# Unit 8's x by the DMA crossbar and the sinks' rows of v by four GpSimd transfers, with a rewritten order of work

## The chip, the cores and the metric

The kernel runs on one core of one Trainium2 chip. Five engines work side by side: TensorE (PE) multiplies matrices, VectorE (DVE) and ScalarE (ACT) work element by element, GpSimd (POOL) does the same more slowly and can issue transfers, and SyncE (SP) issues most transfers. The metric is the device time of one execution in microseconds. The profile is of one execution, taken by the hardware profiler.

## The reference

Two parts follow each other. The first is attention with a window and sinks, for 4 batches (called images below), 8 heads, 768 positions and 64 channels per head. A query sees the keys of its own and the 127 positions before it, and the first 4 positions of the sequence, the sinks:

```python
scores = scale * np.matmul(q, k.transpose(0, 1, 3, 2))
keep = is_sink | in_window          # is_sink: pos < 4; in_window: 0 <= q - k < 128
a = softmax(np.where(keep, scores, -1e9))
attn_out = np.matmul(a, v)          # heads side by side: x, [4, 768, 512]
```

The second is a channel mix with a hidden width of 1024:

```python
xk = mu_k * x + (1 - mu_k) * x_prev      # x_prev: x one position earlier
xr = mu_r * x + (1 - mu_r) * x_prev
k = np.maximum(xk @ w_k, 0)
out = sigmoid(xr @ w_r) * ((k * k) @ w_v)
```

## The kernel before

The work is cut into 12 units of 256 positions, three for each image: unit u is third `T = u % 3` of image `b = u // 3`. A unit passes through four functions.

- `prepare` (line 528) casts q, k and v from f32 to bf16 and turns q and k so that channels lie on partitions. For units in the lists `KD` and `QD` the turn is a crossbar transpose that SP issues (line 562); for the others it is four PE transposes into a PSUM bank (line 576) and an evacuation by ACT or DVE (line 589). For the first unit of an image it also makes the sinks' keys and values.
- `attend` (line 686) makes scores (line 721), exponentials (ACT, line 775), the mask (DVE, line 789), the product with v (PE, line 808), the reciprocal and the scaled x (DVE, lines 822 and 825). In units 0 and 1, which are in `BIAS`, the mask is added by products with `ident` (line 728). In the second and third unit of an image the sinks come in by scores with `ksink` (line 696), an exponential (line 703) and a product with `vsink` (line 763).
- `mix` (line 834) turns x. For units in `XD` SP issues two crossbar transposes (line 869); for the others it is two halves of four PE transposes each (line 849) and two evacuations (line 858). Then DVE makes the difference `td` of x and x one position earlier (line 877) and the mixes xk and xr, eight instructions (line 888).
- `ffn` (line 928) makes the key products with w_k (line 939), relu (lines 949 or 953), the square (lines 963 or 967), the gate with w_r (line 979) and tanh (line 985), the product with w_v (line 997), the output (line 1006) and the store (line 1013). The last 128 positions go in two column halves (`last_product`, lines 909 to 924).

**The sinks' values before.** `vsink` is a [128, 8 heads, 65] tile that is zero except in the rows where a head finds its four sink positions. A PE product of v's first 128 rows with the constant `spread` (line 676) brings the four sink rows of v to those partitions in a PSUM bank, and DVE multiplies the bank by the mask `hmask` into `vsink` (line 680). Both happen once for each image. `spread` is made by POOL from `ident` (line 451). The keys' counterpart `ksink` is filled by POOL copies (line 670).

**The order.** Each engine works through its own queue in order. The program first records every operation with a number (`Plan.op`), and then emits them in the order of the table `ORDER`. A negative number there is a fill: a product of zeros (line 1018) into a bank that is free at that place. `CHOICE` names the engine where an operation could go to more than one, and `SLOTS` the buffer for each tile. Nothing is decided while the kernel runs; a queue stands still until its next instruction's inputs and buffers are there. SP's queue holds the loads, the crossbar transposes and the stores in one order, so that a transpose that waits for its input keeps what stands behind it waiting.

Of the kernel before, what the change touches and what calls it, by code (L numbers as in the profile page):

```python
# [18 lines left out]
    92: "ACT", 93: "ACT", 94: "ACT", 95: "ACT", 97: "ACT", 100: "ACT", 102: "DVE", 105: "DVE",  # L19
    110: "DVE", 111: "DVE", 114: "ACT", 115: "DVE", 139: "POOL", 142: "POOL", 145: "POOL", 148:  # L20
    "DVE", 150: "DVE", 151: "ACT", 152: "ACT", 154: "DVE", 161: "DVE", 191: "DVE", 193: "DVE",
    194: "DVE", 197: "DVE", 199: "DVE", 200: "DVE", 203: "DVE", 204: "DVE", 213: "DVE", 230:
    "ACT", 234: "ACT", 273: "DVE", 276: "DVE", 279: "DVE", 282: "DVE", 285: "ACT", 286: "ACT",
    298: "DVE", 306: "DVE", 315: "ACT", 354: "DVE", 364: "ACT", 365: "DVE", 367: "DVE", 383:
    "ACT", 387: "ACT", 436: "DVE", 439: "DVE", 444: "DVE", 445: "DVE", 467: "ACT", 475: "ACT",
    514: "DVE", 516: "DVE", 521: "DVE", 524: "ACT", 525: "ACT", 546: "ACT", 550: "ACT", 554:
    "ACT", 558: "ACT", 595: "DVE", 598: "DVE", 603: "ACT", 604: "ACT", 606: "DVE", 634: "ACT",
    681: "DVE", 682: "DVE", 691: "DVE", 700: "ACT", 704: "ACT", 708: "ACT", 755: "DVE", 759:
    "DVE", 760: "ACT", 772: "DVE", 781: "ACT", 785: "ACT", 789: "ACT", 834: "DVE", 836: "DVE",
    837: "DVE", 853: "ACT", 856: "DVE", 857: "ACT", 860: "DVE", 861: "ACT", 904: "DVE", 906:  # L30
    "DVE", 910: "DVE", 912: "DVE", 913: "DVE", 929: "ACT", 933: "ACT", 940: "DVE", 941: "ACT",
    994: "DVE", 995: "ACT", 999: "ACT", 1003: "ACT", 1007: "ACT", 1022: "DVE", 1026: "DVE",
    1034: "DVE", 1035: "ACT",
# [5 lines left out]
XD = (9,10,11)  # L39
# [146 lines left out]
def kernel(  # L186
# [209 lines left out]

    xts = [tile1([128, NC, S + 16], BF16, f"xt{i}") for i in range(2)]
    ones = tile1([128, 128], BF16, "ones")

    def fill():  # L400
        for t, value in ((ones, 1.0), (spread, 0.0), (hmask, 1.0)):
            nc.vector.memset(t, value)
# [672 lines left out]
```

## Time and profile before

| | |
|---|---|
| median of 3 runs | 166.04 us (165.84 to 166.12) |
| span of the profiled execution | 164.3 us; no other time of this execution is given |
| PE busy | 158.4 us, 96% |
| DVE busy | 145.4 us, 89% |
| ACT busy | 131.2 us, 80% |
| POOL busy | 13.5 us, 8% |
| mean granted TensorE clock | 0.999 |

The span runs from the first to the last instruction. In a group of instructions, the line, the engine and the operation come first, then the tiles written and read, the count, the busy time in us, the mean ns of one, and the idle time of the engine ahead of them with what ended it. In a timeline, the first two numbers are the start and the length in us. Busy times of PE are modelled to each matmul's end, and matmuls overlap, so the distance from one start to the next tells what a matmul holds PE for.

### The profile page before, as it was taken

To read this page: it belongs to the slowest core of one execution; us is meant where nothing else is said; L and a number is where in the kernel's file an instruction comes from. 1 tells how busy PE (TensorE), PEld (TensorE's weight loads), DVE (VectorE), ACT (ScalarE), POOL (GpSimd) and SP (SyncE) were. 2 spreads that over 40 slices of the span, in tenths; PEclk is the share of its full clock that TensorE was granted. 3 is DMA by queue.
4 is the path that set the end of the run, shared out by engine and by line. 5 is a ranking of instruction groups with operands and counts; after the bars stand their busy time and mean duration, and the time that the engine had idled before them with its cause. 6 is when DMAs were issued, how large, how long until landed. Compare 5 with 4: busy or idle time off the path is not lost.

```text
span 164.3 us, 4195 instructions
## 1 busy us (share of the span) xinstructions
PE 158.4 (96%) x1603; PEld 102.6 (62%) x1603; DVE 145.4 (89%) x381; ACT 131.2 (80%) x218; POOL 13.5 (8%) x38
## 2 busy tenths in 40 slices
PE   6999889999999999999999999999999999999992
PEld 2455568866467587577566775856575765664851
DVE  5259999999999999989999999999999999789752
ACT  3277999999999999999999999997668759163240
POOL 6409300010000000060000000000000000000000
PEclk9999999999999999999999999999999999999999
DMA  4999999999969896999999887986996955077743
GB/s 120 247 305 311 348 335 355 301 354 210 228 154 270 135 240 148 234 198 167 224 216 157 188 156 163 235 146 150 199 123 136 362 149 200 0 90 297 262 185 128
DMA packets 79042, 34.60 MB, mean 211 GB/s; under 512 B 67112, under 2 KB 73520, under 8 KB 79024
## 3 DMA queue, kind: packets, MB, share of 16 engines
q1 hardware_dynamic: 79008, 34.35, 86.3%
q8 instruction: 12, 0.20, 0.6%
q14 instruction: 6, 0.05, 0.1%
q10 hardware_dynamic: 16, 0.00, 0.0%
HBM read 24.12 MB, written 6.29 MB: 185 GB/s over the span
## 4 chain that ended last, share of the span: by engine, by line
PE 79%; ACT 8%; SPq 4%; DMA 3%; issue 2%; DVE 1%; POOL 1%; DVEq 0%; ACTq 0%; POOLq 0%
PE bank L997 23%; PE bank L939 23%; PE bank L979 12%; PE bank L808 6%; PE sc L721 6%; SPq L337 3%; DMA qs<-in_q_dram 3%; PE bank L576 2%; ACT e L775 2%; PE bank L849 2%; ACT rl L949 1%; PE bank L763 1%; ACT qt L589 1%; PE bank L909 1%; PE bank L1018 1%
## 5 line engine op out<-in xcount | busy, mean ns | idle before, releaser
L775 ACT ACTIVATE e<-sc 128x1024 bf16<-128x1024 f32 (+1 forms) x48 | 46.1, 994 | 1.8 <-PE sc L721 1.7
L939 PE MATMUL bank<-xk,wk_sb 128*128 128x256 bf16 x384 | 47.1, 273 | 0.0
L997 PE MATMUL bank<-wv_h,kk 128*128 128x512 bf16 x184 | 43.1, 379 | 0.1
L939 PEld LDWEIGHTS <-wk_sb 128*128 128x128 bf16 x384 | 36.4, 98 | 7.4 <-issue 0.4
L949 ACT ACTIVATE rl<-bank 128x512 bf16<-128x512 f32 x40 | 24.2, 625 | 8.6 <-PE bank L939 7.1
L997 PEld LDWEIGHTS <-kk 128*128 128x128 bf16 x184 | 17.1, 98 | 17.8 <-issue 0.4
L789 DVE TENSOR_TENSOR e<-e,mask 128x1024 bf16<-128x1024 bf16 (+1 forms) x40 | 25.4, 642 | 0.7 <-ACT e L775 0.5
L979 PE MATMUL bank<-wr_sb,xr 128*128 128x512 bf16 x96 | 23.7, 379 | 0.0
L888 DVE SCALAR_TENSOR_TENSOR xk<-td,mu_all,xt 128x256 bf16<-128x256 bf16 x48 | 22.4, 483 | 0.3
L888 DVE SCALAR_TENSOR_TENSOR xr<-td,mu_all,xt 128x256 bf16<-128x256 bf16 x48 | 22.1, 475 | 0.2
L967 ACT ACTIVATE kk<-rl 128x512 bf16<-128x512 bf16 x29 | 18.3, 664 | 4.2 <-DVE rl L953 4.0
L985 ACT ACTIVATE th<-bank 128x512 f32<-128x512 f32 x24 | 15.1, 646 | 5.7 <-PE bank L979 5.7
L825 DVE TENSOR_TENSOR x<-bank,rec 128x256 bf16<-128x256 f32 x48 | 19.2, 416 | 0.4
L808 PE MATMUL bank<-vb,e 128*128 128x65 bf16 x352 | 16.6, 194 | 0.0
L1006 DVE SCALAR_TENSOR_TENSOR w<-th,bank 128x512 f32<-128x512 f32 x19 | 13.0, 682 | 3.6 <-issue 1.8
L808 PEld LDWEIGHTS <-e 128*128 128x128 bf16 x352 | 13.6, 97 | 3.5
L979 PEld LDWEIGHTS <-xr 128*128 128x128 bf16 x96 | 8.8, 98 | 8.6 <-issue 0.2
L721 PE MATMUL sc<-qt,kt 64*128 64x128 bf16 (+1 forms) x256 | 13.9, 238 | 0.0
L721 PEld LDWEIGHTS <-kt 64*128 64x128 bf16 x256 | 8.9, 94 | 5.7 <-issue 3.1
L1018 PE MATMUL bank<-warm 128*128 128x512 bf16 x30 | 10.6, 484 | 1.1 <-DVE warm L1038 1.1
L877 DVE TENSOR_TENSOR td<-xt 128x512 bf16<-128x512 bf16 x24 | 10.3, 428 | 0.7 <-ACT xt L858 0.5
L589 ACT COPY qt<-bank 128x512 bf16<-128x512 bf16 x15 | 9.4, 643 | 1.0 <-PE bank L576 1.0
(74 smaller groups left out, 161.7 us busy)
## 6 DMA issues: line engine op xcount, KB each, us to landing
ks<-in_k_dram SPq DMA_DIRECT2D x24, 256.0 KB, 4.7
qs<-in_q_dram SPq DMA_DIRECT2D x24, 256.0 KB, 4.4
vs<-in_v_dram SPq DMA_DIRECT2D x24, 256.0 KB, 4.4
out_dram<-w SPq DMA_DIRECT2D x19, 256.0 KB, 2.7
w<-in_moe_w_k_dram SPq DMA_DIRECT2D x2, 1024.0 KB, 10.4
w<-in_moe_w_v_dram SPq DMA_DIRECT2D x2, 1024.0 KB, 9.3
w<-in_moe_w_r_dram SPq DMA_DIRECT2D x1, 1024.0 KB, 9.7
out_dram<-ob SPq DMA_DIRECT2D x4, 256.0 KB, 2.6
```

Source lines behind the costliest of these rows:

```text
L721: nc.tensor.matmul(out=sc[:, a, o0:o1], lhsT=lhs[rows], rhs=rhs[rows], start=u not in BIAS, stop=True, skip_group_check=u in BIAS)
L775: nc.scalar.activation(out=buf[ek][:, :, lo:], in_=buf[sck][:, :, lo:], func=AF.Exp, scale=scale)
L789: nc.vector.tensor_tensor(out=at, in0=at, in1=m, op=ALU.mult)
L808: nc.tensor.matmul(out=o[:, g, a, :], lhsT=e[:, a, e0:e0 + 128], rhs=rhs, start=(T == 0 and i == 0), stop=(i == len(blocks) - 1), skip_gro ...
L825: P.op("DVE", dve(256), lambda ok=ok, rk=rk, c=c: nc.vector.tensor_tensor(out=buf["x", u][:, :, 128 * c:128 * c + 128].rearrange("p g (a d ...
L888: nc.vector.scalar_tensor_tensor(out=buf[key][:, c, :], in0=buf[tk][:, i, :], scalar=mu[w][:, c:c + 1], in1=xt[:, c, t0 - 1:t0 + 255], op0 ...
L939: nc.tensor.matmul(out=ps[:, i, :], lhsT=wk_sb[:, c, 128 * f:128 * f + 128], rhs=xk[:, c, :], start=(c == 0), stop=(c == NC - 1), skip_gro ...
L949: nc.scalar.activation(out=buf[rk], in_=buf[psk].rearrange("p (i t) -> p i t", i=2), func=AF.Relu)
L967: nc.scalar.activation(out=buf["kk", u][:, 2 * f2:2 * f2 + 2, :], in_=buf[rk], func=AF.Square)
L979: nc.tensor.matmul(out=buf[psk], lhsT=buf["xr", u][:, c, 128 * g:128 * g + 128], rhs=wr_sb[:, c, :], start=(c == 0), stop=(c == NC - 1))
L985: P.op("ACT", act(512), lambda psk=psk, tk=tk: nc.scalar.activation(out=buf[tk], in_=buf[psk], func=AF.Tanh, scale=0.5), rank + 4 + g, tak ...
L997: nc.tensor.matmul(out=buf[psk], rhs=wv_h[:, f, :], lhsT=buf["kk", u][:, f, 128 * g:128 * g + 128], start=(f == 0), stop=(f == NF - 1))
```

## The change

- `XD` takes in unit 8. Its x is turned by two crossbar transposes that SP issues, and its eight PE transposes and two evacuations are gone.
- `spread` and the four products with it are gone. A new tile `vstage` (f32, [128, 4, 64]) is set to zero by DVE, and then four transfers issued by POOL write the sinks' rows of v for all four images at once: transfer i brings position i of every head and image to partitions i, i + 16, and so on, 8 partitions and 32 rows of 256 bytes. `vsink` is the product of `vstage` (spread over the heads) and `hmask`, read from SBUF; it can go to POOL or DVE, and `CHOICE` gives all four to DVE. `hmask` and `ksink` follow the new places of the rows (16 apart for the two heads of a pair, not 4).
- The sinks' keys of image 1 are followed by 18 POOL writes of zero, of one element per partition, to an unused tile `spare`.
- `ORDER`, `CHOICE` and `SLOTS` are rewritten. SP loads q ahead of k for units 0 and 1. Fills go from 30 to 24. On POOL, units 0 and 1 get three more casts (half of v of unit 0, both of unit 1). Of the relus 2 are on DVE, where 8 were; of the squares 26, where 19 were; of v's casts 7, where 13 were; of q's casts 8, where 14 were. The first and the last quarter of w_k are cast by DVE, where all four were ACT's.

The core of the diff (the three tables are left out; their effect stands above):

```diff
-XD = (9,10,11)
+XD = (8, 9, 10, 11)
...
-    spread = tile1([128, 128], BF16, "spread")
...
+    vstage = tile1([128, B, D], FP32, "vstage")
...
+    spare = tile1([128, 18], FP32, "spare")
...
-        for t in ksink + vsink:
+        for t in ksink + vsink + [vstage]:
             nc.vector.memset(t, 0.0)
...
-            keep(m, -4 * a, [[-32, NP], [0, D + 1]], 1, m)
-            keep(m, 3 + 4 * a, [[32, NP], [0, D + 1]], -1, m)
+            keep(m, -16 * a, [[-32, NP], [0, D + 1]], 1, m)
+            keep(m, 3 + 16 * a, [[32, NP], [0, D + 1]], -1, m)
...
+    for i in range(NS):
+        P.op("POOL", 1000.0, lambda i=i: nc.gpsimd.dma_start(
+            out=vstage[i::16], in_=v[:, :, i, :].rearrange("b h d -> h b d")), -50,
+            service=60.0, descs=32, reads=["stage0"], writes=[("vstage", i)])
...
-                nc.gpsimd.tensor_copy(out=kz[rows, :, 4 * a:4 * a + NS],
+                nc.gpsimd.tensor_copy(out=kz[rows, :, 16 * a:16 * a + NS],
                                       in_=first(rows))
+            if b == 1:
+                for i in range(18):
+                    nc.gpsimd.memset(spare[:, i:i + 1], 0.0)
...
-        psk = ("vsp", b)
-        P.op("PE", 220.0, lambda: nc.tensor.matmul(
-            out=buf[psk].rearrange("p (h d) -> p h d", h=H), lhsT=spread,
-            rhs=buf["vb", u][:, 0, :, 0:D], start=True, stop=True), rank + 4, lag=PE_LAG,
...
-        P.op("DVE", dve(512), lambda: nc.vector.tensor_tensor(
...
+        def sink_values(engine):
+            return lambda: engine.tensor_tensor(
+                out=vsink[b % 2][:, :, 0:D], op=ALU.mult, in1=hmask[:, :, 0:D],
+                in0=vstage[:, b, :].unsqueeze(1).to_broadcast([128, H, D]))
+
+        P.op("POOL", 1250.0, sink_values(nc.gpsimd), rank + 4, port=True,
+             alts={"POOL": (1250.0, sink_values(nc.gpsimd), True),
+                   "DVE": (dve(512), sink_values(nc.vector), True)},
+             reads=[("vstage", i) for i in range(NS)] + ["hmask", "sinks"],
+             writes=[("vsink", b % 2)])
```

More of the change, by code (lines that the diff above doesn't have):

```diff
@@ L18 @@
 CHOICE = {
[L19 to L30, printed above, removed]
@@ L31 @@
-    "DVE", 910: "DVE", 912: "DVE", 913: "DVE", 929: "ACT", 933: "ACT", 940: "DVE", 941: "ACT",
-    994: "DVE", 995: "ACT", 999: "ACT", 1003: "ACT", 1007: "ACT", 1022: "DVE", 1026: "DVE",
-    1034: "DVE", 1035: "ACT",
+    95: "DVE", 96: "ACT", 97: "ACT", 98: "DVE", 99: "DVE", 100: "ACT", 101: "DVE", 102: "DVE",
+    103: "ACT", 104: "DVE", 105: "DVE", 107: "ACT", 108: "ACT", 110: "DVE", 111: "DVE", 113:
+    "DVE", 114: "ACT", 116: "ACT", 117: "DVE", 118: "POOL", 120: "DVE", 141: "POOL", 143: "ACT",
@@ new lines @@
+    144: "DVE", 146: "ACT", 147: "POOL", 149: "ACT", 150: "POOL", 152: "ACT", 153: "POOL", 154:
+    "POOL", 156: "DVE", 163: "DVE", 193: "DVE", 195: "ACT", 196: "DVE", 198: "ACT", 199: "DVE",
+    201: "DVE", 202: "ACT", 204: "ACT", 205: "DVE", 206: "ACT", 208: "ACT", 215: "ACT", 223:
+    "ACT", 224: "ACT", 227: "ACT", 228: "DVE", 231: "DVE", 232: "ACT", 235: "ACT", 236: "ACT",
+    275: "DVE", 277: "ACT", 278: "DVE", 280: "ACT", 281: "DVE", 283: "ACT", 284: "DVE", 286:
+    "ACT", 287: "ACT", 288: "ACT", 290: "DVE", 292: "DVE", 299: "DVE", 307: "ACT", 308: "DVE",
@@ new lines @@
+    311: "ACT", 312: "DVE", 315: "ACT", 316: "ACT", 319: "ACT", 320: "DVE", 355: "DVE", 357:
+    "ACT", 359: "ACT", 360: "ACT", 362: "ACT", 364: "ACT", 365: "ACT", 366: "DVE", 368: "DVE",
+    375: "ACT", 383: "ACT", 384: "ACT", 387: "ACT", 388: "ACT", 391: "ACT", 392: "DVE", 395:
+    "ACT", 396: "DVE", 435: "ACT", 437: "DVE", 439: "ACT", 440: "DVE", 442: "ACT", 444: "ACT",
+    445: "DVE", 446: "DVE", 448: "ACT", 455: "DVE", 463: "ACT", 464: "DVE", 467: "ACT", 468:
+    "DVE", 471: "ACT", 472: "DVE", 475: "ACT", 476: "ACT", 515: "ACT", 517: "ACT", 519: "ACT",
@@ L34 @@
+    934: "ACT", 937: "ACT", 938: "DVE", 991: "ACT", 992: "ACT", 995: "DVE", 996: "DVE", 999:
+    "ACT", 1000: "DVE", 1003: "ACT", 1004: "DVE", 1019: "ACT", 1020: "DVE", 1023: "ACT", 1024:
+    "DVE", 1027: "ACT", 1028: "ACT", 1031: "ACT", 1032: "DVE",
 }
@@ L395 @@
     vsink = [tile1([128, H, D + 1], BF16, f"vsink{i}") for i in range(2)]
+    vstage = tile1([128, B, D], FP32, "vstage")
     xts = [tile1([128, NC, S + 16], BF16, f"xt{i}") for i in range(2)]
     ones = tile1([128, 128], BF16, "ones")
+    spare = tile1([128, 18], FP32, "spare")
     def fill():
-        for t, value in ((ones, 1.0), (spread, 0.0), (hmask, 1.0)):
+        for t, value in ((ones, 1.0), (hmask, 1.0)):
             nc.vector.memset(t, value)
@@ L414 @@
     const_op("DVE", 500.0, fill, ["ones0"], rank=-80)
-    const_op("DVE", 1800.0, fill_later, ["sinks0", "ones", "edges"], rank=-79)
+    const_op("DVE", 1800.0, fill_later, ["sinks0", "stage0", "ones", "edges"], rank=-79)
     def keep(out, base, pattern, multiplier, in_=ones, fill=0.0):
@@ L446, in make_bias1 @@
         window_mask(early.bitcast(BF16)[:, 384:640], warm[:, 0:128], LOW)
-    def make_spread():
-        for a in range(2):
-            nc.gpsimd.tensor_copy(
-                out=spread[0:NS, :].rearrange("p (c w) -> p c w", w=32)[:, :, 4 * a:4 * a + NS],
-                in_=ident[0:NS, 0:NS].unsqueeze(1).to_broadcast([NS, NP, NS]))
     def make_hmask():
@@ L479 @@
     const_op("POOL", 1250.0, make_mask0, ["mask0"], ["ones0"], rank=-55)
-    const_op("POOL", 200.0, make_spread, ["spread"], ["ident", "ones0"], rank=-54)
     const_op("POOL", 1400.0, make_hmask, ["hmask"], ["ones0"], rank=-53)
@@ L669, in sink_keys @@
                 rows = slice(64 * a, 64 * a + 64)
-                nc.gpsimd.tensor_copy(out=kz[rows, :, 4 * a:4 * a + NS],
+                nc.gpsimd.tensor_copy(out=kz[rows, :, 16 * a:16 * a + NS],
                                       in_=first(rows))
+            if b == 1:
+                for i in range(18):
+                    nc.gpsimd.memset(spare[:, i:i + 1], 0.0)
         P.op("POOL", 500.0, sink_keys, rank + 4, hold=[("kt", u)], port=True,
              reads=["sinks", ("kt", u, 0), ("kt", u, 1)], writes=[("ksink", b % 2)])
-        psk = ("vsp", b)
-        P.op("PE", 220.0, lambda: nc.tensor.matmul(
-            out=buf[psk].rearrange("p (h d) -> p h d", h=H), lhsT=spread,
-            rhs=buf["vb", u][:, 0, :, 0:D], start=True, stop=True), rank + 4, lag=PE_LAG,
-            take=[("bank", psk)], hold=[("vb", u)], reads=["spread", ("vb", u, 0)], writes=[psk])
-        P.op("DVE", dve(512), lambda: nc.vector.tensor_tensor(
-            out=vsink[b % 2][:, :, 0:D], op=ALU.mult, in1=hmask[:, :, 0:D],
-            in0=buf[psk].rearrange("p (h d) -> p h d", h=H)), rank + 4, hold=[psk],
-            reads=[psk, "hmask", "sinks"], writes=[("vsink", b % 2)])
+        def sink_values(engine):
[7 more added lines that the diff above has]
+             writes=[("vsink", b % 2)])
     def attend(u, rank):
```

12 lines of the change are left out of this document (added), and 157 rows, old and new, of tables (ORDER, SLOTS).

## The prediction

> **What bounds the kernel now.** I read the page's busy shares and chain first, then the busy time by stage, then TensorE's own timeline.
>
> ```profile
> span 164.3 us, 4195 instructions
> PE 158.4 (96%) x1603; PEld 102.6 (62%) x1603; DVE 145.4 (89%) x381; ACT 131.2 (80%) x218; POOL 13.5 (8%) x38
> ...
> PE 79%; ACT 8%; SPq 4%; DMA 3%; issue 2%; DVE 1%; POOL 1%; DVEq 0%; ACTq 0%; POOLq 0%
> ```
>
> ```profile
> 0.00:24.00 24.00, 21.48 (x217) 11.69 (x218) 16.75 (x54) 16.31 (x26) 9.86 (x32) 1.00 0.94 277
> 24.00:110.00 86.00, 85.85 (x944) 58.70 (x944) 83.22 (x219) 85.27 (x146) 3.62 (x6) 1.00 0.97 215
> 110.00:140.00 30.00, 30.00 (x305) 18.91 (x304) 29.35 (x75) 22.02 (x36) 0.00 (x0) 1.00 0.81 184
> 140.00:161.20 21.20, 21.11 (x145) 13.34 (x142) 15.70 (x36) 7.59 (x13) 0.00 (x0) 1.00 0.53 165
> ```
>
> After the time come the busy times of PE, weight loads, DVE, ACT and POOL, then clock, DMA share and GB/s. From 24 to 161.2 us TensorE is never visibly idle at a granted clock of 1.00, while DVE and ACT are over 95% busy until 110. Since matmul ends are modelled, I checked this by counting: adding each PE operation of the written order at the start-to-start distance of its kind (a 256-column matmul 0.109 us, a 512-column one 0.216, as the rows below give) makes 136.1 us from the first key product to the end. The trace takes 23.98 to 161.11 (rows below), 137.1 us. So only about 1.0 us of that stretch is waiting. The end is: when the dense stretch starts, plus the PE work in it, plus its waits, plus a tail of 3.2 us. The first 24 us also hold most of the PE work that only fills time, zero products:
>
> ```profile
> L1018 PE MATMUL bank<-warm 128*128 128x512 bf16 x30 | 10.6, 484 | 1.1 <-DVE warm L1038 1.1
> ```
>
> The sum is made on this execution's span. The page gives no other time of it; the median, 166.04, is 1.74 above the span, and I carry that difference over unchanged.
>
> **The change, part by part.**
>
> PE work taken out of the dense stretch:
>
> ```profile
> 50.35 0.62 PE L721 MATMUL sc<-qt,kt 64*128 64x256 bf16 x12
> 50.90 1.05 PE L939 MATMUL bank<-xk,wk_sb 128*128 128x256 bf16 x8
> 51.79 0.38 PE L676 MATMUL bank<-vb,spread 128*128 128x512 bf16 x1
> 52.01 1.03 PE L979 MATMUL bank<-wr_sb,xr 128*128 128x512 bf16 x4
> ```
>
> ```profile
> 23.98 1.05 PE L939 MATMUL bank<-xk,wk_sb 128*128 128x256 bf16 x8
> 24.87 0.39 PE L849 MATMUL bank<-ident,x 128*128 128x128 bf16 x4
> 25.09 0.39 PE L576 MATMUL bank<-ident,kb 128*128 128x128 bf16 x4
> ```
>
> The product with `spread` holds PE for 52.01 - 51.79 = 0.22 us; three of four lie in the dense stretch: -0.66. The transposes of x take 25.09 - 24.87 = 0.22 for each half; unit 8 has two: -0.44. Together **-1.10**. The fourth product lies in the first 24 us, among fills.
>
> Work moved ahead of the dense stretch: the new order has the second transpose of x of unit 1 (0.22) and the first scores of unit 2 (50.90 - 50.35 = 0.55) before `keys0.0.0`, not behind it: **-0.77**, if the start stays. Six fills go; they only bridged waits, and cost nothing to lose.
>
> The start itself. The cast of the first quarter of w_k goes from ACT to DVE, where it stands behind the difference `td` of unit 1, and that waits for ACT to evacuate unit 1's x:
>
> ```profile
> 22.85 1.08 ACT L501 ACTIVATE wk_sb<-w 128x1024 bf16<-128x1024 f32 x1
> 23.80 0.61 ACT L858 COPY xt<-bank 128x512 bf16<-128x512 bf16 x1
> ```
>
> ```profile
> L949 ACT ACTIVATE rl<-bank 128x512 bf16<-128x512 f32 x40 | 24.2, 625 | 8.6 <-PE bank L939 7.1 <-ACT kk L967 0.9 <-ACT rl L949 0.2
> L877 DVE TENSOR_TENSOR td<-xt 128x512 bf16<-128x512 bf16 x24 | 10.3, 428 | 0.7 <-ACT xt L858 0.5
> L967 ACT ACTIVATE kk<-rl 128x512 bf16<-128x512 bf16 x29 | 18.3, 664 | 4.2 <-DVE rl L953 4.0
> L963 DVE TENSOR_TENSOR kk<-rl 128x512 bf16<-128x512 bf16 x19 | 7.7, 416 | 0.0
> L953 DVE TENSOR_SCALAR rl<-bank 128x512 bf16<-128x512 f32 x8 | 5.5, 685 | 1.5 <-PE bank L939 1.5
> L646 DVE CAST vb<-vs 128x512 bf16<-128x512 f32 x13 | 5.4, 420 | 0.1
> L507 DVE CAST wr_sb<-w 128x1024 bf16<-128x1024 f32 x1 | 0.7, 682 | 0.0
> ```
>
> Until that evacuation ACT's list is nearly as long as it was up to 22.85 (two evacuations and a cast come, two v casts and one exp of the sinks go), so I put it at 22.95; +0.61, +0.43 for `td`, +0.68 for the cast (the w_r row has its shape) and 0.1 of hand-over: key products from about 24.75 in place of 23.98. **+0.77**. So what moved ahead is paid by a later start. Bounds: 0, if ACT gets there 0.8 earlier, to +1.5.
>
> The vector engines. Six relus go from DVE to ACT, seven squares the other way; six casts of v leave DVE (three to POOL), a net six of q go to ACT. DVE: -6 x 0.685 + 7 x 0.416 - 12 x 0.42 = -6.2, and some 0.7 comes back by w_k casts and others: -5.5 us. ACT: +6 x 0.625 - 7 x 0.664 + casts, about +2. The four multiplies by `hmask` stay on DVE (all four choices say so), now from SBUF. With PE the bound this is slack: 0 on the path; at best it removes the 1.0 us of waits, at worst a reordered in-order queue adds as much.
>
> The GpSimd transfers. No such issue is in the trace. POOL now runs the same three masks first, then four issues, `sinks`, and half of unit 0's v cast, for which the first products with v wait:
>
> ```profile
> 0.81 0.55 ACTq L374 DMA_DIRECT2D ob<-in_moe_mu_r_dram  x1
> 4.68 0.30 POOL L434 MEMSET ob<- 4x256 bf16 x1
> 11.06 0.34 PE L808 MATMUL bank<-vb,e 128*128 128x65 bf16 x6
> 12.64 0.86 POOL L543 CAST qb<-qs 128x512 bf16<-128x512 f32 x1 [6.67 <-DMA qs<-in_q_dram]
> 15.74 0.55 POOL L470 COPY vsink<-hmask 128x8 bf16<-128x8 bf16 x2
> ```
>
> The masks end near 4.9 (here 4.98). With i for one issue the cast ends at 4.9 + 4i + 0.55 + 0.86, and the product starts at 11.06: free up to i = 1.16. The nearest rows are the small issue on ACT, 0.55, and a crossbar transpose on SP, median 1.23 (below); a queue's waiting issue took 2.4 there. I take 1.0, nearer the transpose since software must write descriptors, an estimate: **0**. The 18 single-element POOL writes behind the sinks' keys of image 1 cost about 18 x 0.1 and nobody waits: POOL is busy 3.62 of 86 us.
>
> The Trainium skill, SBUF — State Buffer, section "SBUF: two separate sides", speaks against this: while DVE runs a two-port copy, GpSimd cannot write its descriptors. By it the four early DVE casts (about 0.43 each) could hold the issues up by 1.7 us in all, and the cast would be some 1 us late: 166.3 where the sum gives 165.3. No run here shows it yet.
>
> The crossbar for unit 8:
>
> ```profile
> L869 SPq DMA_TRANSPOSE xt<-x x6: 1189/1230/2405, 117.3 to 144.0; - x6
> ...
> DMA to landing us min/median/max: 2.5/3.5/4.2
> ```
>
> Two issues, then landing: x complete near 110 (counted along PE's new order), landed by 110 + 1.23 + 3.5 = 114.7, about 3.4 us of DVE work, and its first key product is due near 121: hidden by prod6, prod7 and scores, **0**. Without that cover it would be 4.7 against a transpose and copy on PE and ACT of about 1. Behind it on SP stand the last half of q11, a transpose, and v10's second half (a rival below). The copies saved on ACT and DVE are counted above.
>
> The tail. In the old order 10 long PE steps of 0.864 and 8 of 0.437 stand between the last product with v and the keys of unit 11:
>
> ```profile
> 139.88 0.40 PE L808 MATMUL bank<-vb,e 128*128 128x65 bf16 x8
> 142.34 0.42 DVE L825 TENSOR_TENSOR x<-bank,rec 128x256 bf16<-128x256 f32 x1
> 142.79 3.65 SPq L869 DMA_TRANSPOSE xt<-x  x2
> 147.88 0.42 DVE L877 TENSOR_TENSOR td<-xt 128x512 bf16<-128x512 bf16 x1
> 152.25 3.66 PE L939 MATMUL bank<-xk,wk_sb 128*128 128x256 bf16 x32
> 159.20 1.91 PE L909 MATMUL bank<-wv_h,kk 128*128 128x256 bf16 x16
> ```
>
> That is 12.1 us of cover. In the new order 7 of each: 9.1. The chain behind that product: x complete 2.2 later (DVE's new list), second transpose issued after 1.23, landed after 3.5, two `td` and four mixes about 2.5 (DVE now does all xk before xr), 0.1: 9.5. **+0.4**; bounds 0 and +2.
>
> Sum: -1.10 - 0.77 + 0.77 + 0.4 = -0.7: 165.3 us. q ahead of k loads the same bytes before w_k: 0, within 0.5 either way.
>
> **The rivals.** (A) Slower: the GpSimd issues hold POOL. From i = 1.16 on, everything in its queue is late, v0, then q1's and k1's casts, which feed unit 1's scores. At i = 2 the cast ends at 14.3, 3.3 us late, and ACT, which carries unit 1 to the dense stretch, has little idle time to swallow it:
>
> ```profile
> 15.00:20.00 5.00, 4.54 (x60) 2.67 (x58) 5.00 (x14) 4.42 (x8) 2.87 (x10) 1.00 1.09 336
> ```
>
> 0.58 of 5 us there: 3.3 - 0.6 = 2.7 late: 168.0. For it: four issues in a row ahead of needed work. Against: 32 rows each.
> (B) No change: v10's second half is issued behind unit 8's transposes, near 115.
>
> ```profile
> L307 SPq DMA_DIRECT2D vs<-in_v_dram x24: 572/592/3568, 3.6 to 125.4; - x24
> ...
> DMA to landing us min/median/max: 3.2/4.4/9.6
> ```
>
> At the median landing and a cast on ACT, taken as a relu's 0.63, it is there at 120.1, and its product is due near 120.6: it just fits. At 5.6 to landing the gain is gone: 166.0; at 9.6, 170. For it: DMA is the shared resource, busy 0.97 up to 110. Against: the old order issues v10 earlier but also waits at SP for unit 9's x, and PE shows no gap there.
> (C) Larger gain: ACT is early, the start stays at 24.0 and some waits go: -1.10 - 0.77 - 0.2: 164.0. PE's work alone caps it: 23.98 + 134.2 + 3.2 + 1.74 = 163.1.
>
> **How the numbers follow.** Forecast 0.47, C 0.17, A 0.18, B 0.18. A change under 0.2% (0.33 us) can't be told from none. The forecast's own range is 164.8 to 166.0 and mostly lies under 165.7 (0.40 of 0.47); C is faster; B is half same, half slower; A slower. Faster 0.57, same 0.16, slower 0.27. The range runs from near C, 163.7, to near A, 167.2; the likeliest one's is 164.8 to 166.0.
>
> **What would show it.** Right: PE busy without gaps from about 24.7 to 160; POOL's v cast ended before 11; key products of unit 11 start with under 0.5 us of wait. Wrong: PE waiting for POOL near 10 to 17 us (A), for v10 near 120 (B), or key products at 24 us or earlier (C). A span outside 162 to 165.5 would mean that a step was missed.

## The result: the same median, a lower floor and a wide spread

| | median | lowest to highest | runs |
|---|---|---|---|
| kernel before | 166.04 us | 165.59 to 166.75 | 12 |
| changed kernel | 165.88 us | 163.60 to 167.00 | 12 |

The ratio after to before is 0.9909 (95% interval 0.9882 to 0.9936). The ratios of this document leave out runs more than 1.5% above the fastest of their kernel, and since the longer runs of the changed kernel show the same granted clock as its others (0.998 or more in all of them), the medians of all runs stand beside them. By the medians the change is worth 0.16 us, nothing that can be told from none. What did change is the spread: 1.2 us before, 3.4 us after. Three more series of the changed kernel, on three chips, are told below. All 42 of its runs have a median of 166.2 us, with the middle half from 164.9 to 167.0; the 71 runs of the kernel before beside them have 166.27, middle half 166.0 to 166.6.

The page of the changed kernel, of an execution that took 166.16 us, answers the lines shown of before:

```profile
span 164.5 us, 4166 instructions
...
PE 154.9 (94%) x1567; PEld 101.0 (61%) x1585; DVE 141.5 (86%) x371; ACT 132.3 (80%) x223; POOL 17.6 (11%) x61
...
PE 65%; DMA 11%; DVE 3%; ACT 1%; issue 1%; SPq 0%; DVEq 0%
PE bank L1013 20%; PE bank L955 20%; PE bank L995 9%; DMA w<-in_moe_w_v_dram 8%; PE bank L824 5%; PE sc L737 4%; DMA out_dram<-ob 3%; PE bank L588 2%; PE bank L865 1%; PE bank L925 1%; PE bank L779 1%; DVE xr L904 1%; PE bank L712 1%; DVE e L805 1%; ACT wv_h L513 1%
```

PE is busy 3.5 us less and the span is 0.2 us longer. A part of the 3.5 is not real: this trace lacks 18 of PE's 1585 matmul records (compare the counts of PE and of weight loads), and the complete trace of the same program further down has PE busy for 156.0 us. In the chain of waits, transfers went from 3% to 11%, 8% of it the load of w_v: the chain now runs through the landing of a weight. The busy time by stage says where PE stood (columns as before; the second row is the one that was 85.85 of 86):

```profile
0.00:24.00 24.00, 20.79 (x225) 11.67 (x225) 17.32 (x55) 15.79 (x25) 13.04 (x37) 1.00 0.95 275
24.00:110.00 86.00, 83.11 (x902) 57.23 (x912) 81.71 (x211) 82.40 (x143) 4.58 (x24) 1.00 1.06 218
110.00:140.00 30.00, 29.74 (x313) 18.75 (x315) 28.43 (x75) 25.94 (x43) 0.00 (x0) 1.00 0.69 142
140.00:161.40 21.40, 21.26 (x137) 13.34 (x137) 13.66 (x32) 8.19 (x15) 0.00 (x0) 1.00 0.62 224
```

Nearly 3 us of PE's time are missing between 24 and 110 us (a part of it again by the records that are not there), and little behind that. The list of what PE waited for from 12 us on begins with these places, which together make 2.2 us:

```profile
PE bank L1013 <- ACT wv_h L513: 1.1, 1, 1.1
PE bank L995 <- ACT es L719: 0.7, 1, 0.7
PE bank L955 <- ACT rl L965: 0.4, 1, 0.4
```

The longest is a product with w_v that waits for the cast of w_v, and that cast waits for the load. These rows of the timeline hold the start of the dense stretch, that wait and the last product:

```profile
23.45 1.06 ACT L513 ACTIVATE wk_sb<-w 128x1024 bf16<-128x1024 f32 x1 [0.73 <-DMA w<-in_moe_w_k_dram]
...
24.20 1.92 PE L955 MATMUL bank<-xk,wk_sb 128*128 128x256 bf16 x16 [0.17 <-DVE wk_sb L519]
...
43.31 1.06 ACT L513 ACTIVATE wv_h<-w 128x1024 bf16<-128x1024 f32 x1 [1.52 <-DMA w<-in_moe_w_v_dram]
...
159.46 1.91 PE L925 MATMUL bank<-wv_h,kk 128*128 128x256 bf16 x16
```

The prediction's sum can be read off them. The dense stretch runs from 24.20 to 161.37, 137.2 us. Its PE work is 136.1 - 1.10 - 0.77 = 134.2 by the prediction's count, so 3.0 us of it is waiting, where it was 1.0 (this goes by the ends of the stretch and does not depend on missing records); the tail is 164.5 - 161.37 = 3.1. In this execution the work that was taken out came back as waits.

### The profile page after: what moved, and what is told of

The parts are those of the page before. It is cut to its first block, busy times and chain, and to the rows that moved or that the text cites. A ratio compares the mean times of both kernels' runs of the same rounds, so it can differ in the third digit from the quotient of the medians.

```text
span 164.5 us, 4166 instructions
## 1 busy us (share of the span) xinstructions
PE 154.9 (94%) x1567; PEld 101.0 (61%) x1585; DVE 141.5 (86%) x371; ACT 132.3 (80%) x223; POOL 17.6 (11%) x61
## 4 chain that ended last, share of the span: by engine, by line
PE 65%; DMA 11%; DVE 3%; ACT 1%; issue 1%; SPq 0%; DVEq 0%
PE bank L1013 20%; PE bank L955 20%; PE bank L995 9%; DMA w<-in_moe_w_v_dram 8%; PE bank L824 5%; PE sc L737 4%; DMA out_dram<-ob 3%; PE bank L588 2%; PE bank L865 1%; PE bank L925 1%; PE bank L779 1%; DVE xr L904 1%; PE bank L712 1%; DVE e L805 1%; ACT wv_h L513 1%
## 5 line engine op out<-in xcount | busy, mean ns | idle before, releaser
L791 ACT ACTIVATE e<-sc 128x1024 bf16<-128x1024 f32 (+1 forms) x48 | 44.8, 972 | 2.2 <-PE sc L737 2.1
L965 ACT ACTIVATE rl<-bank 128x512 bf16<-128x512 f32 x46 | 26.3, 612 | 8.2 <-PE bank L955 7.7
L904 DVE SCALAR_TENSOR_TENSOR xk<-td,mu_all,xt 128x256 bf16<-128x256 bf16 x48 | 21.7, 478 | 0.2
L841 DVE TENSOR_TENSOR x<-bank,rec 128x256 bf16<-128x256 f32 x48 | 19.8, 418 | 0.7
L1001 ACT ACTIVATE th<-bank 128x512 f32<-128x512 f32 x24 | 14.5, 617 | 4.1 <-PE bank L995 4.0
L824 PE MATMUL bank<-vb,e 128*128 128x65 bf16 x352 | 17.2, 194 | 0.5 <-ACT e L791 0.5
L983 ACT ACTIVATE kk<-rl 128x512 bf16<-128x512 bf16 x22 | 14.0, 660 | 0.0
L1022 DVE SCALAR_TENSOR_TENSOR w<-th,bank 128x512 f32<-128x512 f32 x17 | 11.5, 681 | 2.6 <-PE bank L1013 1.8
L682 POOL COPY ksink<-kt 64x16 bf16<-64x16 bf16 x8 | 4.3, 534 | 83.3 <-DVE kb L548 34.5
L979 DVE TENSOR_TENSOR kk<-rl 128x512 bf16<-128x512 bf16 x26 | 10.4, 415 | 1.7 <-ACT rl L965 1.7
```

What stands on the lines that cost most here:

```text
L791: nc.scalar.activation(out=buf[ek][:, :, lo:], in_=buf[sck][:, :, lo:], func=AF.Exp, scale=scale)
L824: nc.tensor.matmul(out=o[:, g, a, :], lhsT=e[:, a, e0:e0 + 128], rhs=rhs, start=(T == 0 and i == 0), stop=(i == len(blocks) - 1), skip_gro ...
L841: P.op("DVE", dve(256), lambda ok=ok, rk=rk, c=c: nc.vector.tensor_tensor(out=buf["x", u][:, :, 128 * c:128 * c + 128].rearrange("p g (a d ...
L904: nc.vector.scalar_tensor_tensor(out=buf[key][:, c, :], in0=buf[tk][:, i, :], scalar=mu[w][:, c:c + 1], in1=xt[:, c, t0 - 1:t0 + 255], op0 ...
L965: nc.scalar.activation(out=buf[rk], in_=buf[psk].rearrange("p (i t) -> p i t", i=2), func=AF.Relu)
L983: nc.scalar.activation(out=buf["kk", u][:, 2 * f2:2 * f2 + 2, :], in_=buf[rk], func=AF.Square)
```

## The experiments

The question was where the 1.87 us of PE work went, and whether one part of the change costs what another gains. Theory L, formed from the traces, says that the new order of loads brings the weights late. Its rivals were that the median is the chip's own noise, that one of the two parts (the crossbar, the GpSimd transfers) carries the effect, and that a faster PE simply meets loads that were never faster (theory M). In the diffs below the long tables are written by the names of their entries: `ld_k3.1` is the second half of the load of k of unit 3, `turn_` and `turnx` are crossbar transposes.

**The changed kernel again**, three times, on three chips, as control for its neighbours. There is no edit.

> The changed kernel once more, to see which of its times comes with which waits. Theory L (the loads of w_r and w_v, late behind k3 and v2 in SP's queue, make its times differ): in a run near 164 us the second half of w_v is there before 42 us and TensorE waits under 1.5 us between 24 and 110 us; in a run near 166 it lands near 43.3 and TensorE waits near 2.9 us there, as in the first profile. Rival (the reordered queues of ACT and DVE make the difference): the waits differ elsewhere, after 60 us, with w_v at the same place.

> The changed kernel beside the next three on one chip. By theory L (it waits for w_r or w_v between 33 and 45 us, by how long the loads take this time) its times spread over 2 us or more, and the profile shows a TensorE wait on a cast of w_r or w_v.

> The changed kernel as it is, as the control for the three beside it. Earlier its median was 165.9, 166.45 and 166.07, its single times from 163.6 to 168.0. Both theories: median 165.5 to 166.5, ratio to the kernel before 0.990 to 0.998.

Measured: medians 166.45 (164.72 to 167.97, 12 runs; ratio 0.9966, 0.9931 to 1.0002), 166.07 (163.69 to 166.98, 9 runs; 0.9910, 0.9863 to 0.9957) and 166.71 (163.24 to 169.54, 9 runs; 0.989, 0.9844 to 0.9936). The spread stays on all three chips, 3.3 to 6.3 us where the kernel before beside it has 1.1 to 1.7, so it belongs to the kernel. The second of them was profiled in one of its quick executions, 163.69 us, and that shows what the others lose. Its timeline and its busy time by stage:

```profile
22.96 0.59 ACT L874 COPY xt<-bank 128x512 bf16<-128x512 bf16 x1
...
23.67 0.42 DVE L893 TENSOR_TENSOR td<-xt 128x512 bf16<-128x512 bf16 x1
...
24.00 0.68 DVE L519 CAST wk_sb<-w 128x1024 bf16<-128x1024 f32 x1
...
24.75 1.92 PE L955 MATMUL bank<-xk,wk_sb 128*128 128x256 bf16 x16
...
41.37 1.06 ACT L513 ACTIVATE wv_h<-w 128x1024 bf16<-128x1024 f32 x1
...
156.97 1.91 PE L925 MATMUL bank<-wv_h,kk 128*128 128x256 bf16 x16
```

```profile
24.00:110.00 86.00, 86.00 (x943) 59.12 (x941) 84.23 (x219) 84.80 (x147) 4.32 (x24) 1.00 1.10 224
```

In these rows no cast of a weight waits for its load, PE is busy in the whole stretch, and 24.75 to 158.88 is 134.13 us: the counted work with no wait at all. The start is *later* than in the execution of 166.2 us. The granted clock is 1.00 in both. So what separates 163.7 from 166.2 us is not the start but the waits behind it.

The other two controls show where else such waits lie. In the first, an execution of 165.02 us, the longest is 0.73 us, for the cast of w_r, which waited for its load; w_v's cast came at 42.06. In the third, of 166.16 us, the list begins with other places:

```profile
PE bank L995 <- ACT es L719: 0.7, 1, 0.7
PE bank L955 <- DVE ob L1022: 0.5, 1, 0.5
```

They stand at 68.83 and 123.56. Compared start by start with the quick execution, PE loses 0.7 us up to 44 us there and 1.6 us behind 60 us. So the weights are not the whole of it, and the wait on a cast of w_r or w_v that theory L expected does not lead this list. A transfer is near both places all the same: ACT's cast of q had waited 0.90 us for its load at 65.96, and the output `ob`, which makes the bank of the second wait free, had itself waited 0.85 us for a store in the first control (121.70).

**Each part alone, on the kernel before.** First the crossbar for unit 8, with before's order otherwise: SP's transposes stand where x is complete, and seven mixes of unit 8 move behind unit 9's first scaled x.

```diff
-XD = (9,10,11)
+XD = (8, 9, 10, 11)
 ORDER (SP):
-  ld_k11.1 turn_q10.0 turn_q10.1 ld_v10.0 turn_k10.1 ...
+  turnx8.1 turnx8.0 ld_k11.1 turn_q10.0 turn_q10.1 ld_v10.0 turn_k10.1 ...
```

> The kernel before with its own order, only unit 8's x by the crossbar: 2 x 0.22 us of TensorE work and two copies less. Theory P (TensorE's work sets the end): 0.44 us less, 165.6. Rival Q (the old order has as much cover as it needs, and what is taken from TensorE turns into a wait): no change within 0.3 us; if SP's queue suffers from the two transposes, up to 1 us more.

Measured: 173.18 us (172.30 to 173.59, 6 runs), ratio 1.0403 (1.0365 to 1.0440). The timeline of this kernel shows why:

```profile
110.08 2.50 SPq L864 DMA_TRANSPOSE xt<-x  x2
...
113.30 2.52 SPq L557 DMA_TRANSPOSE qt<-qb  x2
...
116.56 1.42 SPq L557 DMA_TRANSPOSE kt<-kb  x1
...
117.19 0.29 PE L691 MATMUL bank<-qt,ksink 128*32 128x256 bf16 x4 [2.77 <-DVE xr L883]
...
119.97 0.82 PE L716 MATMUL sc<-qt,kt 64*128 64x128 bf16 x10 [2.27 <-DMA kt<-kb]
```

SP issues in order and stood until unit 8's x was there at 110.08; q and k of unit 10, which wait behind it, were turned 5 to 6 us later than in before, and PE, out of work, waited for them. (The list names a mix of DVE for the first wait; the second transpose of q landed at 117.05.) What costs here is not seen to be the crossbar itself but what stands in SP's queue behind a transpose that waits. The rewritten order puts unit 8's transposes behind those of unit 10's q and k (112.53 in the changed kernel, with no wait on PE in that execution). Its queue is therefore part of what makes this edit free. A later place in before's own order was not tried, so it is not shown that the rest of the rewritten order is needed for it.

Next the four GpSimd transfers alone, on before's order, without the 18 writes to `spare`:

```diff
-  POOL: spread     PE: sinkvals0..3 (product with spread)     DVE: multiply from PSUM
+  POOL: bias1 vstage2 vstage3 vstage0 vstage1                  DVE: multiply vstage by hmask
```

> The kernel before with its own order, only the sinks' rows of v by four GpSimd transfers (issued after the masks, where GpSimd idles), without the 18 single-element writes: four products with spread less, three of them in the dense stretch. Theory P: 0.66 us less, 165.4. Rival Q: no change within 0.3 us. If the transfers as such cost something outside the engines' queues (before the first or after the last instruction), it shows here as more.

Measured: 166.04 us (165.66 to 166.81, 12 runs), ratio 0.9987 (0.9963 to 1.0011), beside 166.23 of before. Four PE products of 0.22 us are gone, three of them in the dense stretch, and about 0.2 us shows in the time, less than can be told from nothing. The spans show more. Their median is 163.9 us, where the runs of before beside it have 164.4, and in the profiled execution the dense stretch takes 136.55 us in place of 137.1: the 0.66 us arrive, nearly. But 2.09 us of each time lie outside the span, where before has 1.87 (means of 12 and 23 runs). The profile does not reach there, and the changed kernel with the same four transfers has 1.70, so the cause is open. Both parts together on before's order:

> The kernel before with its own order and both of these parts, so all that the change takes from TensorE, without the rewritten order. Theory P: 1.1 us less, 164.9; what the changed kernel gains or loses beyond that is the order's. Rival Q: within 0.3 us of before, and the whole gain is the order's.

Measured: 173.03 us (171.41 to 173.79, 6 runs), ratio 1.0386 (1.0338 to 1.0434), as the first part alone. The diff is the sum of the two above. No run comes near 163.7 us without the rewritten order.

**The price of a GpSimd issue.** Each of the four transfers is issued three times, twice into tiles that nobody reads, so that POOL has twelve issues where it had four. The computation is not changed by this.

```diff
-            out=vstage[i::16], in_=...)
+            out=to[i::16], in_=...) for to in (vmore[0], vmore[1], vstage)]
```

> The changed kernel with each GpSimd transfer issued three times, twice into tiles that nobody reads: 12 issues of about 0.57 us in place of 4, so that GpSimd is free for unit 0's v cast near 12.0 in place of 7.4. Theory A (from the point where that cast is late, GpSimd sets the first units): the cast ends near 12.6, the first product with v starts 2 us later than at 10.53, and 1.5 us or more reach the end. Rival (the first 24 us have slack in their fills): the first product is as late, but under 0.5 us reach the end.

Measured: 169.05 us (168.37 to 170.44, 6 runs), ratio 1.0167 (1.0125 to 1.0209). The tile's own view (duration in ns: least, median, most) in the changed kernel, and then in this one, and under them rows of this kernel's timeline:

```profile
L493 POOL DMA_DIRECT2D vstage<-in_v_dram x4: 541/544/688, 4.7 to 6.5; - x4
...
DMA to landing us min/median/max: 4.1/4.6/5.3
```

```profile
L492 POOL DMA_DIRECT2D vmore<-in_v_dram x8: 541/543/698, 4.7 to 11.7; - x8
```

```profile
8.10 0.70 POOL L492 DMA_DIRECT2D vmore<-in_v_dram  x1
8.26 0.43 DVE L555 CAST kb<-ks 128x512 bf16<-128x512 f32 x1 [4.64 <-DMA ks<-in_k_dram]
...
10.61 0.54 POOL L492 DMA_DIRECT2D vstage<-in_v_dram  x1 [1.29 <-DMA vmore<-in_v_dram]
...
13.68 0.46 PE L824 MATMUL bank<-vb,e 128*128 128x65 bf16 x10 [2.18 <-POOL vb L658]
...
29.45 1.92 PE L955 MATMUL bank<-xk,wk_sb 128*128 128x256 bf16 x16
```

An issue costs 0.54 us of POOL, the first one 0.69, not the 1.0 assumed. With twelve, the ninth also stood 1.29 us until an earlier transfer had landed. POOL's cast of v is late, PE waits 2.18 us for it, and the lateness of 3.1 us runs on and grows to 4.7 at the first key product, 29.45 in place of 24.75. Some of that growth falls in a stretch of low granted clock, 0.52 from 14 to 16 us and 0.63 from 16 to 18. At the end it is still there: the span is 166.6 us against 162.0 of the quick execution (the medians are 3.0 us apart). So the mechanism of rival A exists here, and with four issues its price kept it from deciding.

**Weights earlier in SP's queue.** Theory L in its first form blamed k of unit 3 and v of unit 2, which the new order puts ahead of w_r. Two kernels move the weights forward:

```diff
 a_w1:
-  ... ld_k3.1 ld_v2.0 ld_v2.1 ld_wr ...  ld_k4.0 ld_wvb ...
+  ... ld_k3.1 ld_v2.0 ld_wr ld_v2.1 ...  ld_wvb ld_k4.0 ...
 a_w2:
-  ... ld_k3.1 ld_v2.0 ld_v2.1 ld_wr ld_q3.0 ld_q3.1 ld_wva ld_k4.0 ld_wvb ...
+  ... ld_k3.1 ld_wr ld_v2.0 ld_v2.1 ld_q3.0 ld_wva ld_q3.1 ld_wvb ld_k4.0 ...
```

> The changed kernel with two loads moved in SP's queue: w_r ahead of the last half of v2, and the second half of w_v ahead of k4, as the old order had them. Theory L: w_r and w_v land 0.6 to 1 us earlier, TensorE's wait for them between 30 and 45 us (0.73 in one profile, 1.10 in the other) goes, the spread of the times shrinks to about that of the kernel before, and the median falls by 0.7 to 1.5 us against the changed kernel beside it. Rival (the loads are only the first of several waits in a row, and ACT and DVE are what is short): under 0.3 us.

> The same, further: w_r ahead of both halves of v2, the first half of w_v ahead of the last half of q3, the second ahead of k4. Theory L: like the run before or better by up to 0.5 us, as long as v2 and q3 still come in time; if v2 is late, TensorE waits for the products with v of unit 2 near 30 us instead, and the time is no better than the changed kernel's. Rival: under 0.3 us.

Measured: 166.13 us (164.26 to 168.37, 8 runs; ratio 0.9916, 0.9884 to 0.9949) and 167.56 us (165.12 to 169.15, 12 runs; 0.9989, 0.9955 to 1.0023), against the unchanged 166.07 on that chip. The weights' waits went, and v of unit 2 took their place, here in the first of the two:

```profile
33.23 0.62 ACT L656 CAST vb<-vs 128x512 bf16<-128x512 f32 x1 [1.45 <-DMA vs<-in_v_dram]
33.90 0.52 PE L822 MATMUL bank<-vb,e 128*128 128x65 bf16 x12 [1.43 <-ACT vb L656]
```

That form of the theory fell. Moving one load forward makes another the late one: from 23 to 44 us the DMA engines have no room left (share 0.99 and 1.01 in these two).

**The order of loads put back.** In the changed kernel SP now takes the seventh to thirty-third load (`a_load`), or the seventh to eighteenth, up to w_k (`a_early`), in before's order. Unit 0 keeps q ahead of k, and everything else of the change stays.

```diff
 a_load, a_early:
-  ld_q1.0 ld_q1.1 ld_k1.0 ld_k1.1 ld_q2.0 ld_q2.1 ld_v1.0 ld_v1.1 ld_k2.0 ld_k2.1 ld_wka ld_wkb
+  ld_k1.0 ld_q1.0 ld_q1.1 ld_k1.1 ld_v1.0 ld_q2.0 ld_q2.1 ld_k2.0 ld_k2.1 ld_v1.1 ld_wka ld_wkb
 a_load only:
-  ld_k3.0 ld_k3.1 ld_v2.0 ld_v2.1 ld_wr ld_q3.0 ld_q3.1 ld_wva ld_k4.0 ld_wvb ld_k4.1 ...
+  ld_v2.0 ld_k3.0 ld_k3.1 ld_wr ld_v2.1 ld_q3.0 ld_q3.1 ld_wva ld_wvb ld_k4.0 ld_k4.1 ...
```

> The changed kernel, but SP issues the loads of units 1 to 4 and of the weights in the order of the kernel before (seventh to thirty-third load); unit 0's loads, every other instruction and every engine's choice stay as they are. Theory L (the new order of loads brings the weights late): the first half of w_k is issued at 13.5 to 14.0 in place of 14.9 to 15.7, w_r and w_v are waited for under 0.4 us each, and the time is 163.6 to 164.5 in nearly all runs, ratio 0.982 to 0.988. Theory M (the loads of the first 44 us run at the full DMA rate in either order, and TensorE, with 1.87 us less of work, simply reaches them): the issue of w_k moves, but the last load to land before 44 us is waited for as before, 1 to 3 us in all; 165.5 to 166.5 with single times spread over 2 us or more.

> The changed kernel with the order of loads of the kernel before up to w_k only (seventh to eighteenth load); from there on the changed kernel's order, k of unit 3 and both halves of v of unit 2 ahead of w_r. Theory L, if the loads ahead of w_k are its cause: w_k is issued at 13.5 to 14.0 and the time is 163.6 to 164.5, as with the whole order put back. Theory L, if it is k of unit 3 and v of unit 2 ahead of w_r: w_k early, but w_r and w_v still waited for, 165 to 166. Theory M: 165.5 to 166.5.

Measured: 164.54 us (164.00 to 165.56, 6 runs; ratio 0.9892, 0.9863 to 0.9921) and 165.17 us (164.95 to 166.33, 6 runs; 0.9928, 0.9902 to 0.9955), on a chip where the changed kernel had 166.71 (163.24 to 169.54) and before 166.48 (165.88 to 167.01). The spread of 6.3 us is down to 1.6, and the median is 2.2 us lower: over six runs, the changed kernel with before's load order is steadily quicker than both. The ratios are alike (0.9892 and 0.989), so what the order put back takes away is the upper part of the spread. Theory M, 165.5 to 166.5 with a spread of 2 us or more, is out. Theory L's numbers are not met either: w_k is issued at 14.5 and 14.1, not 13.5 to 14.0, and the ratio is above 0.988. The trace of the first one shows more (first the weights' own view with the issues of w_k and w_v and the time to landing of all weights, then its timeline):

```profile
L364 SPq DMA_DIRECT2D w<-in_moe_w_k_dram x2: 1004/1417/1830, 14.5 to 15.5; - x2
L364 SPq DMA_DIRECT2D w<-in_moe_w_v_dram x2: 762/1312/1862, 28.2 to 31.0; - x2
...
DMA to landing us min/median/max: 8.4/8.6/10.9
```

```profile
13.68 0.43 DVE L553 CAST qb<-qs 128x512 bf16<-128x512 f32 x1 [1.57 <-DMA qs<-in_q_dram]
13.71 0.86 POOL L553 CAST qb<-qs 128x512 bf16<-128x512 f32 x1 [1.09 <-DMA qs<-in_q_dram]
...
26.47 1.92 PE L953 MATMUL bank<-xk,wk_sb 128*128 128x256 bf16 x16
...
42.83 1.10 ACT L511 ACTIVATE wv_h<-w 128x1024 bf16<-128x1024 f32 x1
...
158.74 1.91 PE L923 MATMUL bank<-wv_h,kk 128*128 128x256 bf16 x16
```

The loads of q come later, their casts wait, and the key products start at 26.47, 1.7 us behind the quick execution of the changed kernel. From there to 160.65 are 134.18 us, again the counted work without a wait. The weights are there in time. The second half of w_v, issued at 31.0, landed 8.6 us later, at 39.6 (before: 39.3); its cast at 42.83 waited for ACT's queue and not for the load. In three executions of the changed kernel that cast waited for the load and could start at 42.06, 42.21 and 43.31. So the order put back brings w_v 2.4 us or more earlier, as theory L has it. But PE also comes later to it: a wait that was behind the start now lies ahead of it, where it may differ less from run to run. In `a_early`, which keeps the new order for w_r and w_v, PE waited for no weight either, with a start at 25.91; the one wait listed behind that start, 0.46 us, is at 122.74, for an output. How much of the 2.2 us is the weights' earlier landing and how much the later start, the runs do not separate. All executions can be written as one sum:

| execution | key products start | waits until the last product | tail | span |
|---|---|---|---|---|
| before | 23.98 | 1.0 | 3.2 | 164.3 |
| changed | 24.20 | 3.0 | 3.1 | 164.5 |
| changed, first control | 24.47 | 1.5 | 3.1 | 163.3 |
| changed, second control | 24.75 | 0.0 | 3.1 | 162.0 |
| changed, third control | 24.80 | 2.3 | 3.1 | 164.4 |
| order up to w_k put back | 25.91 | 0.4 | 3.1 | 163.6 |
| whole order put back | 26.47 | 0.0 | 3.1 | 163.7 |
| twelve GpSimd issues | 29.45 | 0.0 | 3.1 | 166.6 |

The waits are what is left over: the stretch from the start to the end of the last product, less 136.1 us of work in the first row and 134.2 in the others. In the last row the tail is taken over and the wait follows from the span.

**The new order of loads on the kernel before** was to show the order's price by itself.

```diff
 b_load (kernel before):
-  ld_k1.0 ld_q1.0 ld_q1.1 ld_k1.1 ld_v1.0 ld_q2.0 ld_q2.1 ld_k2.0 ld_k2.1 ld_v1.1 ld_wka ...
+  ld_q1.0 ld_q1.1 ld_k1.0 ld_k1.1 ld_q2.0 ld_q2.1 ld_v1.0 ld_v1.1 ld_k2.0 ld_k2.1 ld_wka ...
```

> The kernel before, but SP issues the seventh to thirty-third load in the order of the changed kernel; the rest stays. Theory L: w_k is issued 1 to 1.5 us later than 13.6, the rate of 5 to 23 us falls from some 318 GB/s to some 300, and TensorE waits for weights 0.5 to 1.5 us more: 166.7 to 168, ratio 1.003 to 1.012. Theory M: the order costs nothing to the slower work of the kernel before: 165.8 to 166.5, ratio within 0.002 of 1. Either: SP's new order was not made for the casts of this kernel, so a wait of a cast of unit 1 or 2 before 24 us can add up to 1 us more.

In this kernel the cast of the fourth quarter of w_v stands ahead of that quarter's load and takes what w_k left in the buffer, so the last part of w_v is not the reference's, and the load then waits for the cast, until 44.4 us, with all of SP's queue behind it. Its 174.32 us (173.79 to 177.09, 6 runs; ratio 1.0478, 1.0440 to 1.0517) are the price of that and say nothing about the order. What can be read is its trace up to 23 us, where it differs from before by the order of loads alone. The busy time of that stage (last column GB/s) and the issues of w_k, first in the kernel before and then in this one:

```profile
5.00:23.00 18.00, 16.73 (x192) 9.83 (x191) 13.27 (x37) 13.66 (x23) 6.20 (x17) 1.00 1.06 318
```

```profile
L354 SPq DMA_DIRECT2D w<-in_moe_w_k_dram x2: 676/1310/1943, 13.6 to 14.3; - x2
```

```profile
5.00:23.00 18.00, 16.22 (x180) 9.31 (x179) 11.91 (x34) 13.12 (x21) 5.84 (x17) 1.00 1.02 282
```

```profile
L349 SPq DMA_DIRECT2D w<-in_moe_w_k_dram x2: 505/556/606, 15.6 to 16.3; - x2
```

The DMA engines are nearly as busy as before (1.02 and 1.06), but move 282 GB/s in place of 318, and w_k, with the same loads ahead of it, is issued 2.0 us later. This is one execution; the changed kernel shows the same in four (276 to 307 GB/s, w_k at 14.9 to 15.7), and the GpSimd transfers on before's order do not (315 GB/s, 13.7). With the order put back in the changed kernel it is 300 and 303 GB/s, and w_k at 14.5 and 14.1: part of the delay goes, and the rates lie within those of the new order. So the order of these loads moves w_k, but it is not the only thing that does.

## Why the prediction was right, and where it was not

The forecast was 165.3 us, and the range 163.7 to 167.2 holds the 165.88 measured. That it came so near is partly luck: it was a sum of one figure per term, and the kernel has no single figure for one of them. Its likeliest outcome, faster (0.57), is what the ratio says; by the medians of all runs it is the same, which had 0.16. And by its own sign, a span outside 162 to 165.5, a step was missed: 10 of the 42 spans lie outside.

- **The frame** (start, PE work, waits, tail) can be laid on every trace, since the waits are what is left over. What bears it out is that nothing is left over in the executions in which PE shows no long wait. The 1.74 us outside the span that were carried over are near, but not the same on both sides: 1.87 for before and 1.70 for the changed kernel (means of 59 and 42 runs). So 0.17 us of the change lies where the profile does not reach.
- **PE work taken out, -1.10, and moved ahead, -0.77**: right to 0.1 us. 136.1 - 1.87 = 134.23 was counted; the two executions without waits took 134.13 and 134.18.
- **The start, +0.77**: right, link by link, in the quick execution: the evacuation at 22.96 (22.95 was said), `td` from 23.67 for 0.42, the cast from 24.00 for 0.68, products at 24.75. In the profile of the result the evacuation was earlier, the cast waited for the load of w_k until 23.45, and the start was 24.20. The bound of 0 to +1.5 holds all four profiled starts.
- **"q ahead of k loads the same bytes before w_k: 0, within 0.5 either way"**: this is the step that failed. The bytes are the same, but w_k is issued 1.4 to 2.2 us later, and w_v's second half, behind k of unit 4 in the new order, lands 2.7 us or more later in three of four executions. The prediction then carried the 1.0 us of waits over from before, with a bound of 1.0 either way; they are 0 to 3.0 us, different in each execution. The term lies outside its bound and is the largest of the sum.
- **Vector engines, 0 on the path**: by the busy times of the page DVE fell by 3.9 us and ACT rose by 1.1, less than the 5.5 and 2 that were worked out, but with the signs said. Behind 44 us PE waits 0.7 us for an exponential of ACT in the first profile (the row with `es` above), but in the third control it loses 1.6 us there, beyond the bound of 1.0. A load of q and, in the first control, a store come just ahead of these waits, so how much the reordered queues cost by themselves is not shown.
- **GpSimd issues, 0**: right, with i = 0.54 in place of 1.0. The first product with v came at 10.54, where it was 11.06.

```profile
9.90 0.61 POOL L658 CAST vb<-vs 128x512 bf16<-128x512 f32 x1 [2.50 <-DMA vs<-in_v_dram]
...
10.54 0.35 PE L824 MATMUL bank<-vb,e 128*128 128x65 bf16 x6
```

  The cast waited for the load of v, not for the issues. What the Trainium skill says in SBUF — State Buffer, section "SBUF: two separate sides", that GpSimd cannot write descriptors while DVE runs a two-port copy, would have shown as a long issue. The four took 541 to 688 ns, but DVE stood idle beside them until 7.54, so here the rule was not put to the test. With twelve issues, the seventh (8.10 above) ran beside a cast of DVE (8.26) and took 698 ns, where its neighbours took 541 to 544; it ended 0.11 us after that cast. This agrees with the rule, in one case and with 0.16 us. The eighth ran beside a second cast and took 541. So the hold-up that the prediction bounded at 1.7 us is small here, and the late cast did not come.
- **The 18 writes to `spare`, 0**: not tried alone.
- **The crossbar for unit 8, 0**: right, given SP's new order. Its transposes were issued at 112.53, the mixes xk ended at 121.73, and the key products began at 122.71 without a wait. (In the first and the third control products at this place waited 0.2 and 0.5 us, for the output `ob`.) Ahead of unit 10's transposes in before's order it costs 7 us.
- **The tail, +0.4**: it is 0. The last mix xk of unit 11 ended at 147.45 (start 145.78, four of them), and PE shows no wait there. The bound from below, 0, was right.

```profile
145.78 1.67 DVE L904 SCALAR_TENSOR_TENSOR xk<-td,mu_all,xt 128x256 bf16<-128x256 bf16 x4
146.44 3.22 PE L955 MATMUL bank<-xk,wk_sb 128*128 128x256 bf16 x28
```

- **Rival A** (GpSimd issues hold POOL) did not come, but its mechanism is real: twelve issues lengthen the span by 4.6 us against the quick execution, some of it under a lower granted clock. **Rival B** (v10's second half late) did not come: it was issued at 117.04, cast from 120.25, and used at 122.46 without a wait. **Rival C** (164.0, waits gone) is what the quick executions are, 163.7 us and once 163.24; its reason was only half right, since the waits went while the start was late, and its sign, key products at 24 us or earlier, did not come.

The signs to look for misled in one point: "PE busy without gaps from about 24.7 to 160" is true of the quick execution and not of the one profiled first. One profile would have shown either.

What is not settled: why w_k is issued later in the new order with the same bytes ahead of it, why the time at which w_r and w_v land differs by up to 2 us between executions of one kernel, and what takes the different times outside the span.

## What to carry to other kernels

Work taken off the engine that sets the end counts only where its inputs are early: ask of each load ahead of the dense stretch how long it had been there before it was used, since a kernel whose weights land just in time turns a gain into a wait, and a different one in each run. Judge such a change by the spread of many runs and by the profiles of a short and a long execution, not by one. On a queue that issues in order, place a transpose that waits for computed data behind everything whose inputs are ready, or count all that stands behind it.

## What the runs showed of the hardware that was not expected

- On the kernel before, another order of the same loads moved fewer bytes at a nearly unchanged DMA share: 282 GB/s at 1.02 in place of 318 at 1.06 (5 to 23 us, one execution each). On the changed kernel the two orders do not separate by rate (276 to 307 in the new one, 300 and 303 with the old one put back).
- A GpSimd issue of 32 rows of 256 bytes took 0.54 us with four or twelve in a row, the first 0.69, and landed 3.6 to 5.8 us later. In the row of twelve the ninth waited 1.29 us for a landing.
- After PE had idled for half of ten microseconds, its granted clock fell. In the kernel with only the crossbar for unit 8, by stage:

```profile
110.00:120.00 10.00, 4.95 (x48) 2.90 (x48) 6.20 (x18) 4.59 (x9) 0.00 (x0) 0.96 0.62 130
120.00:130.00 10.00, 10.00 (x59) 5.58 (x60) 6.31 (x15) 4.64 (x7) 0.00 (x0) 0.69 0.90 161
```

  PE was busy 4.95 of 10 us, and the clock was 0.69 in the next ten, which then hold the work of some 7, an estimate from that clock. So part of the 7 us that this kernel loses is not the wait itself. In the kernel with twelve GpSimd issues PE was busy for 0.32 us of 12 to 14 us, with no single wait above 2.2 us, and the clock was 0.52 in the next two. The waits of 1 us in the other kernels left it at 1.00.
